# Gated linear attention into a squared-ReLU MLP on one core: the first two pairs of chunks handled differently, and the order of work planned anew

## The chip, the core and the metric

The kernel runs on one core of one Trainium2 chip. A core has five engines that run their own instruction streams and meet at semaphores: TensorE (PE; its weight loads are listed apart as PEld), VectorE (DVE), ScalarE (ACT), GpSimd (POOL) and SyncE (SP), which here only issues transfers. The metric is the device time of one launch in microseconds (us). Before the change three runs took 174.03, 174.82 and 174.83 us, so the median is 174.82.

## The reference

Four batches of eight heads go through a recurrence over 768 steps with 48 channels a head. The result, 3072 rows of 384, goes through an MLP with a squared ReLU.

```python
def _attn_ref(q, k, v, alpha) -> np.ndarray:
    for t in range(S):
        state = alpha[:, :, t, :, None] * state + np.einsum('bhd,bhe->bhde', k[:, :, t], v[:, :, t])
        y[:, :, t] = np.einsum('bhd,bhde->bhe', q[:, :, t], state)

def _moe_ref(x, w_in, w_out) -> np.ndarray:
    h = x @ w_in                      # 384 -> 2048
    r = np.maximum(h, 0.0)
    return ((r * r) @ w_out).astype(np.float32)   # 2048 -> 384
```

All inputs and the output are float32; the kernel multiplies in bf16 and accumulates in float32.

## The kernel before, in words

**Tiling.** The 3072 steps are cut into chunks of 128, and two chunks make a *pair* (`g`, 0 to 11; three pairs to a batch). Instead of stepping through time the kernel works on a whole chunk: decays become running sums of logarithms, the part inside a chunk is a masked product of q and k, and the part from earlier chunks comes from a state of 48 by 48 a head that is carried on.

**Stages of a pair.**
- *loads*: alpha, k, q and v into `RAW` (line 596).
- *decay*: logarithm on ACT, running sums by matmuls with triangles of ones on PE, exponentials on ACT into `ASB`, scaling of k and q on DVE into `QKS`, and the cast of v into `VBF` (`values`, line 617). Pairs 0 and 1 do this by halves of the heads (`decay_half`, line 669).
- *turned*: the scaled q and k are transposed into `QKT`. Pairs 0 to 3 do it on PE, with an eviction from PSUM by ACT or DVE (`turned_half`, line 732, for pairs 0 and 1), the later ones by a transposing DMA.
- *scores*: products of q and k, masked into `PMB`. A mask is applied by DVE directly from PSUM (L797), or ACT first copies the bank to SBUF and DVE multiplies from there (L790 and L792). Which of a pair's four masks go the second way is in `COPIED`.
- *carry*: end products, k times v over each of the two chunks (L816, line 805), from which DVE or POOL makes the next states (L831, L834, L837).
- *mixed*: masked scores times v, plus q times the states (L856), evicted into `XT`. In the later pairs the result is turned back by a DMA.
- *up*: eight units a pair, of six matmuls each (L985), with a ReLU on ACT (L995) and the square on DVE (L997).
- *down*: two groups of 16 matmuls a pair, one for each chunk (`tt`, L1018), evicted by ACT (L1025) and stored.

**Transfers.** SP issues most loads. POOL's queue has the weights in nine pieces: first six (five of `WIN`, in cuts 2, 2, 4, 4 and 4 of 16 columns blocks, then one of `WOUT`), gated on the landing of pair 1's alpha (`PARTS`), then the loads of pair 2 (`QUEUED`), then the last three pieces of `WOUT`.

**The order.** Every operation has a priority: `TABLE` gives an offset for each stage of each pair, `2 * g` is added, and lower comes first. PSUM banks and dependencies are drawn in the order of the stages' priorities, from the pools that `POOLS` names: 0 is four banks, 1 adds `psO0`, 2 adds three more. Then `Program.order` runs the engines through a model in which an engine that is free takes the lowest priority among what is ready, and writes the order down; on the chip it is fixed. The model holds durations, and also the arrival of PE's instructions: they come in blocks of `BLOCK` = 254, the first boundary 56 earlier, and a block is there `FETCH` after the one before was begun, less `CALM` outside a busy period. Where PE would idle before the first down, `fill` puts matmuls on a constant tile (L1004), and 28 of them open the program.

**Banks of the MLP.** The ups alternate between two banks, `psH0` and `psH1`; the first `WIDE` of them may also use `psO0`, which is the accumulator of each pair's first down group.

Of the kernel before, what the change touches and what calls it, by code (L numbers as in the profile page):

```python
# [16 lines left out]
    dict(decay0=-97.00571, decay1=-78.81219, turned0=-80.03886, turned1=-50.01967, scores0=-30.48193, scores1=-47.68772, carry=-27.42287, mixed=-10.34508, up=13.54943, down=5.38323, scale00=46.21211, scale01=15.6952, scale10=-43.7223, scale11=24.38742, ends=-0.19963, values=-0.27295, loads=-207.65325, pair=-201.56601, last=-192.65267),  # L17
    dict(decay0=-75.64812, decay1=-42.50964, turned0=-47.6396, turned1=-36.35059, scores0=-27.54796, scores1=-14.27818, carry=-27.02336, mixed=-9.92749, up=13.91788, down=5.77749, scale00=24.25062, scale01=-73.05864, scale10=28.44156, scale11=53.47468, ends=69.1898, values=-2.51561, loads=-194.30495, pair=-191.20832, last=-172.89529),
    dict(decay=-7.48475, turned=3.12884, scores0=9.47855, scores1=6.55405, carry=1.85699, mixed=10.59462, up=17.47201, down=3.43096, loads=-74.75818),
    dict(decay=9.05655, turned=9.43988, scores0=10.08163, scores1=11.32914, carry=10.39665, mixed=11.89133, up=17.92099, down=4.23853, loads=-73.80479),  # L20
    dict(decay=9.3345, turned=9.43988, scores0=11.74226, scores1=10.89073, carry=10.54465, mixed=12.03376, up=21.0863, down=1.87816, loads=-73.8231),
    dict(decay=8.7564, turned=9.67304, scores0=11.70712, scores1=12.0564, carry=10.89438, mixed=12.21007, up=21.29448, down=1.43236, loads=6.43356),
    dict(decay=8.69387, turned=9.58387, scores0=11.86871, scores1=11.0227, carry=10.77621, mixed=11.96308, up=21.05913, down=2.40841, loads=7.7569),
    dict(decay=9.23435, turned=10.31244, scores0=11.36545, scores1=11.31146, carry=10.85231, mixed=12.13782, up=22.61627, down=2.40841, loads=8.07049),
    dict(decay=9.1013, turned=10.6921, scores0=11.60211, scores1=13.72977, carry=10.17742, mixed=18.09191, up=22.49685, down=2.4227, loads=7.9898),
    dict(decay=9.1013, turned=10.66148, scores0=19.46122, scores1=19.67082, carry=16.52927, mixed=20.05528, up=26.04938, down=2.38036, loads=7.9898),
    dict(decay=17.68176, turned=18.97432, scores0=20.03114, scores1=21.47118, carry=18.7218, mixed=19.83455, up=26.32882, down=2.72559, loads=13.16964, masks=-27.17958),
    dict(decay=17.68176, turned=18.97432, scores0=20.03114, scores1=21.47118, carry=18.7218, mixed=19.83455, up=26.32882, down=2.72559, loads=13.16964),
]
POOLS = [dict(decay=1, turned=2, scores=2, carry=1, mixed=2), dict(decay=0, turned=1, scores=1, carry=1, mixed=0)]  # L30
WEIGHTS = (-75.27555, -73.28278)
TURNED = (0, 1, 2, 3)
BACK = (4, 5, 6, 7, 8, 9, 10, 11)
BEHIND = {6: 4, 7: 6, 8: 6, 9: 7, 10: 7, 11: 9}
RUNS = {10: 16}
WARMUP = (28, 1)
WIDE = 10
# [27 lines left out]
class Program:  # L65
# [1146 lines left out]
```

## Time and profile before

| what | value |
|---|---|
| median of three runs | 174.82 us (174.03 to 174.83) |
| the profiled execution | 174.21 us |
| its span, from first to last instruction | 172.5 us |
| PE busy | 167.6 us, 97% |
| DVE busy | 119.4 us, 69% |
| ACT busy | 116.9 us, 68% |
| POOL busy | 36.4 us, 21% |
| matmuls | 2611 |
| granted TensorE clock | full speed in all slices |

Rows of a profile have the engine, a line of the kernel (L985 is line 985), what is written and read, how many instructions, and times. In the table by stretches a row has the stretch, its length, then busy time and number of instructions of PE, PEld, DVE, ACT and POOL, then granted clock, the share of the DMA engines and GB/s. In the chain of waits and the timeline a row begins with its start and its length in us. A bracket names the idle time ahead of an instruction and what ended it; "issue" means that the profile shows nothing that the engine waited for. In a row for one line, three numbers with slashes are minimum, median and maximum in ns.

### The profile page before, as it was taken

The page shows a single profiled execution, that of the slowest core. Times are in us where ns is not written, and L with a number is a line of the kernel's source. Part 1 is how long each engine was busy: PE and PEld are TensorE (multiplying, and loading weights), DVE is VectorE, ACT ScalarE, POOL GpSimd, SP SyncE. Part 2 cuts the span into 40 slices and gives each one's busy share as a digit, 9 for nine tenths or more (in the row PEclk, how much of TensorE's full clock was granted, in tenths as well). Part 3 has the DMA queues.
Part 4 walks back from the last instruction along what each step waited for, and adds up shares of the span by engine and source line. Part 5 has one row for each costly group of instructions (what it writes and reads, how often), then busy time and mean ns, then how long its engine had stood idle before and what let it go on. Part 6 is the DMA issues. An engine that isn't in the chain of part 4 may idle for free.

```text
span 172.5 us, 6016 instructions
## 1 busy us (share of the span) xinstructions
PE 167.6 (97%) x2611; PEld 123.9 (72%) x2611; DVE 119.4 (69%) x257; ACT 116.9 (68%) x236; POOL 36.4 (21%) x63
## 2 busy tenths in 40 slices
PE   7889999999999999999999999999999999999994
PEld 7457687757777786777777777777776867877763
DVE  7887958964999999578897698289784804423300
ACT  2887679546989685568993794669973556657621
POOL 4079600100012001010142122320512310202220
PEclk9999999999999999999999999999999999999999
DMA  5999999999994999999999999999929343112122
GB/s 138 323 304 171 206 324 238 157 270 287 308 327 113 230 217 261 144 305 196 323 203 234 218 207 252 236 231 332 186 50 160 72 62 62 22 25 49 40 51 91
DMA packets 76314, 32.89 MB, mean 191 GB/s; under 512 B 69632, under 2 KB 75456, under 8 KB 76288
## 3 DMA queue, kind: packets, MB, share of 16 engines
q1 hardware_dynamic: 70384, 25.04, 65.0%
q0 software_dynamic: 5904, 7.47, 21.8%
q8 instruction: 20, 0.33, 0.8%
q14 instruction: 6, 0.05, 0.1%
HBM read 25.17 MB, written 4.72 MB: 173 GB/s over the span
## 4 chain that ended last, share of the span: by engine, by line
PE 95%; DVE 2%; issue 1%; ACT 0%
PE psH L985 36%; PE psO L1018 36%; PE psG L777 4%; PE psO L1004 3%; PE psG L856 2%; PE psG L942 2%; PE psG L816 2%; PE psO L1037 2%; PE psG L932 2%; PE psO L985 2%; DVE qks L696 2%; PE psG L642 1%; PE psG L715 1%; PE psG L681 1%; PE psH L856 1%
## 5 line engine op out<-in xcount | busy, mean ns | idle before, releaser
L995 ACT ACTIVATE rr<-psH 128x512 bf16<-128x512 f32 x92 | 55.3, 612 | 22.6 <-PE psH L985 20.6
L985 PE MATMUL psH<-xt,win 128*128 128x256 bf16 x552 | 70.5, 273 | 0.0
L1018 PE MATMUL psO<-wout,gt 128*128 128x384 bf16 x368 | 70.0, 326 | 0.0
L985 PEld LDWEIGHTS psH<-xt,win 128*128 128x128 bf16 x552 | 52.7, 98 | 11.6 <-DVE xt L900 0.2
L997 DVE TENSOR_TENSOR gt<-rr 128x512 bf16<-128x512 bf16 x96 | 40.3, 434 | 29.6 <-ACT rr L995 29.3
L1018 PEld LDWEIGHTS psO<-wout,gt 128*128 128x128 bf16 x368 | 34.3, 98 | 17.8 <-ACT osb L1025 0.3
L797 DVE TENSOR_TENSOR pm<-psG,mask 128x512 bf16<-128x512 f32 x44 | 27.9, 682 | 3.7 <-PE psG L777 2.9
L971 POOL DMA_DIRECT2D out_dram<-osb x28 | 15.0, 541 | 47.4 <-ACT osb L1025 47.4
L837 POOL TENSOR_TENSOR sbf<-ust,acp 128x192 bf16<-128x192 f32 x13 | 9.0, 689 | 75.3 <-DVE ust L834 75.2
L1025 ACT ACTIVATE osb<-psO 128x384 f32<-128x384 f32 x23 | 11.3, 492 | 14.6 <-PE psO L1018 14.3
L663 DVE TENSOR_TENSOR qks<-raw,asb 128x768 bf16<-128x768 f32 x20 | 18.7, 966 | 2.0 <-ACT asb L652 2.0
L632 DVE TENSOR_TENSOR raw<-raw 128x384 f32<-128x384 f32 x20 | 11.0, 564 | 0.0
L624 ACT ACTIVATE vbf<-raw 128x768 bf16<-128x768 f32 x12 | 10.1, 842 | 0.0
L652 ACT ACTIVATE asb<-psG 128x384 bf16<-128x384 f32 x20 | 9.9, 497 | 0.2
L958 ACT ACTIVATE yb<-psG 128x384 bf16<-128x384 f32 x14 | 6.2, 489 | 4.4 <-PE psG L932 4.4
L777 PEld LDWEIGHTS psG<-qkt 64*64 64x64 bf16 x360 | 5.7, 106 | 4.0 <-issue 2.8
L1004 PE MATMUL psO<-warm 128*128 128x128 bf16 (+1 forms) x41 | 7.4, 347 | 1.1 <-DVE warm L523 1.1
L777 PE MATMUL psG<-qkt 64*64 64x128 bf16 x360 | 8.3, 220 | 0.1
L632 DVE TENSOR_TENSOR raw<-raw,ro 128x384 f32<-128x384 f32 x10 | 5.5, 551 | 0.8 <-DMA raw<-in_q_dram 0.5
L648 ACT ACTIVATE ro<-raw 128x384 f32<-128x384 f32 x10 | 5.2, 524 | 0.6 <-DMA raw<-in_alpha_dram 0.6
L834 DVE TENSOR_TENSOR ust<-psG,sbf 128x192 f32<-128x192 f32 x14 | 4.9, 353 | 0.7 <-POOL sbf L837 0.4
L654 ACT ACTIVATE ro<-ro 128x384 f32<-128x384 f32 x10 | 5.2, 524 | 0.1
(104 smaller groups left out, 137.2 us busy)
## 6 DMA issues: line engine op xcount, KB each, us to landing
raw<-in_alpha_dram SPq DMA_DIRECT2D x11, 384.0 KB, 4.8
raw<-in_k_dram SPq DMA_DIRECT2D x11, 384.0 KB, 5.0
raw<-in_q_dram SPq DMA_DIRECT2D x11, 384.0 KB, 5.6
raw<-in_v_dram SPq DMA_DIRECT2D x11, 384.0 KB, 5.9
out_dram<-osb POOLq DMA_DIRECT2D x28, 96.0 KB, 2.6
out_dram<-osb SPq DMA_DIRECT2D x9, 192.0 KB, 3.9
wout<-in_moe_w_out_dram POOLq DMA_DIRECT2D x4, 384.0 KB, 13.6
win<-in_moe_w_in_dram POOLq DMA_DIRECT2D x3, 384.0 KB, 8.8
```

Of the source, the lines that this page charges most:

```text
L624: add("ACT", lambda act: act.activation(dst, src, AF.Copy), 740, at, reads=raw(r, 2), writes=[("vbf", vb)])
L632: add("DVE", lambda e: e.tensor_tensor(dst, a0, a1, ALU.mult), 470, at_, reads=reads, writes=writes, port=True)
L663: add("DVE", lambda dve, z=z, decays=decays: dve.tensor_tensor(QKS[x][:, z, :, :, 0:D], both(r, z), decays, ALU.mult), 870, at + 0.05 + 0. ...
L777: last = pe.matmul(banks[i, j // 2][0][64 * c:64 * c + 64, col:col + 128].rearrange("p (a b) -> p a b", a=2), QKT[t][64 * i:64 * i + 64, 0 ...
L797: add("DVE", lambda dve, i=i, X=X, ps=ps: dve.tensor_tensor(PMB[m][:, i, 2 * X:2 * X + 2].rearrange("p j n s -> p j (n s)"), ps[:].rearran ...
L971: add(by, lambda e, dst=dst, ps=ps: e.dma_start(dst, OSB[o][ps, :]), 600, at + 0.01 * i, reads=[("osb", o)], dma=("own" if by == "POOL" el ...
L985: last = pe.matmul(ps[:, f * TW:(f + 1) * TW].rearrange("p (c t) -> p c t", c=2), WIN[:, kt, fj * 128:(fj + 1) * 128], XT[:, 2 * (g % NX): ...
L995: add("ACT", lambda act: act.activation(ro, ri, AF.Relu), 480, at, reads=[key], writes=[key, ("rr", r)])
L997: add("DVE", lambda dve: dve.tensor_tensor(gt[:, 2 * u:2 * u + 2, :], rr, rr, ALU.mult), 340, at, reads=[("rr", r)], writes=[("gt", g % NG ...
L1004: last = pe.matmul(psO[1][:, 0:128 * wide].rearrange("p (a b) -> p a b", a=wide), WARM[:], bass.AP(tensor=WARM, offset=0, ap=[[128, 128], ...
L1018: last = pe.matmul(ps[:, 0:DM], GT[g % NGT][:, fj, tt * 128:(tt + 1) * 128], WOUT[:, fj, :], start=(fj == 0), stop=(fj == FT - 1))
L1025: add("ACT", lambda act: act.activation(OSB[o][:], ps[:, 0:DM], AF.Copy), 372, at, reads=[key], writes=[key, ("osb", o)])
```

## The change

What it does:
- `COPIED`: two masks of each of the first two pairs go through an ACT eviction, where it was one.
- `CASTS`: pair 0's cast of v goes from ACT to POOL. `TURNS`: the second half of pair 1's transposes is evicted by DVE, where it was ACT.
- `PARTED`: pair 1's carry is issued as two operations, one for each chunk, each with a priority and a pool of its own. `HALVED` could split the masked product of mixed in the same way, but is off for both pairs.
- `POOLS` has an entry for each half.
- `WIDE` is 16, so all ups of pairs 0 and 1 may use `psO0`.
- `BEHIND`: the loads of pairs 9 and 11 are no longer held behind a transpose, those of 10 are. `OWN`: q of pair 10 is loaded through POOL's queue.
- The model's blocks come later: `FETCH` 5900 for 5200, `CALM` 2200 for 1500. All priorities are new, and so is the order in the whole program.

```diff
-    dict(decay0=-97.00571, ... scores0=-30.48193, scores1=-47.68772, carry=-27.42287, mixed=-10.34508, up=13.54943, ...),
-    dict(decay0=-75.64812, ... scores0=-27.54796, scores1=-14.27818, carry=-27.02336, mixed=-9.92749, up=13.91788, ...),
+    dict(decay0=-146.86488, ... scores0=-97.39775, scores1=-60.74046, carry=-78.79402, mixed=-43.93218, up=-29.78865, ..., carry1=-9.28472),
+    dict(decay0=-76.01398, ... scores0=-34.45505, scores1=-34.33621, carry=-68.21069, mixed=-30.58997, up=-27.20524, ..., carry1=-32.02976),
...
-POOLS = [dict(decay=1, turned=2, scores=2, carry=1, mixed=2), dict(decay=0, turned=1, scores=1, carry=1, mixed=0)]
-WEIGHTS = (-75.27555, -73.28278)
+POOLS = [dict(decay0=1, decay1=2, turned0=1, turned1=1, scores0=0, scores1=0, carry=1, carry1=0, mixed=2), dict(decay0=2, decay1=2, turned0=2, turned1=1, scores0=0, scores1=0, carry=2, carry1=0, mixed=2)]
+WEIGHTS = (-161.5303, -133.27356)
-BEHIND = {6: 4, 7: 6, 8: 6, 9: 7, 10: 7, 11: 9}
+BEHIND = {6: 4, 7: 6, 8: 6, 10: 8}
-WIDE = 10
+WIDE = 16
-CASTS = ('ACT', 'ACT')
+CASTS = ('POOL', 'ACT')
-COPIED = ((1,), (2,))
-TURNS = ('DVE', 'ACT')
+COPIED = ((0, 2), (0, 1))
+TURNS = ('DVE', 'DVE')
+PARTED = (0, 1)
+HALVED = (0, 0)
+OWN = ((10, 1),)
...
-    BLOCK, AHEAD_OF_ALL, FETCH, CALM, BUSY_FROM, BUSY_UNTIL = 254, 56.0, 5200.0, 1500.0, 11200.0, 31000.0
+    BLOCK, AHEAD_OF_ALL, FETCH, CALM, BUSY_FROM, BUSY_UNTIL = 254, 56.0, 5900.0, 2200.0, 11200.0, 31000.0
...
+            if (g, j) in OWN:
+                add("POOL", lambda e, s=s, dst=dst: e.dma_start(dst, s), 950, at + 0.1 * (j != 3),
+                    writes=raw(r, j), dma=f"rawq{r}_{j}", nbytes=TW * HD * 4, rate=pr.LATER, tardy=g >= FIRST)
+                continue
...
-    def carry(g, at, spots=None):
+    def carry(g, at, spots=None, part=None):
         first, final = g % NW == 0, g % NW == NW - 1
-        chunks = [0] if final else [0, 1]
+        chunks = [0] if final else [0, 1] if part is None else [part]
+        name = "carry1" if part else "carry"
...
+            if g < FIRST and PARTED[g]:
+                for c in range(2):
+                    stage(2 * g + o["carry1" if c else "carry"], lambda at, g=g, c=c: carry(g, at, None, c), "carry", g, c)
+            else:
+                stage(2 * g + o["carry"], lambda at, g=g: carry(g, at), "carry", g)
```

More of the change, by code (lines that the diff above doesn't have):

```diff
@@ L19 @@
[L19 to L26, printed above, removed]
@@ new lines @@
+    dict(decay0=-76.01398, decay1=-71.34874, turned0=-46.31235, turned1=-38.30092, scores0=-34.45505, scores1=-34.33621, carry=-68.21069, mixed=-30.58997, up=-27.20524, down=10.34217, scale00=-28.77031, scale01=9.28326, scale10=52.36844, scale11=42.61829, ends=-1.25386, values=-13.06113, loads=-168.76464, pair=-167.45514, last=-149.62032, carry1=-32.02976),
+    dict(decay=-33.84237, turned=-32.51282, scores0=-20.86174, scores1=-31.33323, carry=-19.71539, mixed=-19.02679, up=11.43945, down=16.45818, loads=-136.74137),
@@ L768, in scores @@
         halves = sorted({j // 2 for j in js})
-        banks = {(i, X): bank(POOLS[g]["scores"] if g < FIRST else 0) for X in halves for i in range(2)}
+        banks = {(i, X): bank(POOLS[g]["scores%d" % X] if g < FIRST else 0) for X in halves for i in range(2)}
         def mm(pe):
@@ L820, in mm @@
             return last
-        add("PE", mm, 250, at, reads=[("qks", x, 0, X) for X in range(2)] + [("vbf", vb)],
-            writes=[b[1] for b in banks], form=64, size=32 * len(chunks))
+        add("PE", mm, 250 if part is None else 260, at, reads=[("qks", x, 0, X) for X in range(2)] + [("vbf", vb)],
+            writes=[b[1] for b in banks.values()], form=64, size=32 * len(chunks))
         for c in chunks:
@@ L1116, in bass_gla_recurrent__then__act_relu_squared_kernel @@
             ahead(("decay", g, 0), [("decay", g, 1)])
+            if PARTED[g]:
+                ahead(("carry", g, 0), [("carry", g, 1)])
         ahead(("turned", g), [("decay", g + NQK)])
```

41 lines of the change are left out of this document (27 added, 14 removed).

## The prediction

> **What bounds the kernel now.** I read the page first (busy shares, slices), then the table by stretches, the chain of waits over the first 35 us, and then the rows of single lines. The page:
>
> ```profile
> PE 167.6 (97%) x2611; PEld 123.9 (72%) x2611; DVE 119.4 (69%) x257; ACT 116.9 (68%) x236; POOL 36.4 (21%) x63
> PE   7889999999999999999999999999999999999994
> win<-in_moe_w_in_dram POOLq DMA_DIRECT2D x3, 384.0 KB, 8.8
> ```
>
> PE is the bound. The slices show it below nine tenths only in the first three and in the last, so nothing that speeds another engine up in the middle shortens the run: the change can win only PE time that is idle or spent on filler early, or lose what it adds to PE. The stretches say where that is (us; busy and number of instructions by engine):
>
> ```profile
> 5.08:12.20 7.12, 6.18 (x88) 3.75 (x88) 5.94 (x14) 6.69 (x16) 2.70 (x4) 1.00 1.17 323
> 12.20:16.74 4.54, 4.44 (x159) 3.02 (x160) 3.41 (x9) 3.39 (x6) 4.54 (x6) 1.00 1.24 176
> 16.74:22.30 5.56, 5.21 (x110) 3.89 (x114) 4.70 (x12) 2.77 (x5) 3.33 (x5) 1.00 1.26 206
> 22.30:32.60 10.30, 10.30 (x115) 8.39 (x115) 8.11 (x18) 9.91 (x20) 0.00 (x0) 1.00 1.19 268
> ```
>
> From 22.30 PE is busy 10.30 of 10.30. Ahead of that, part of "busy" is filler (line 1004). The chain of waits (start, length):
>
> ```profile
> 14.43 0.37 PE psG L816 x32
> 14.80 0.54 PE psO L1004 x2
> 16.06 0.32 PE psO L1004
> 16.74 0.83 PE psH L985 x6
> 20.66 0.32 issue
> 20.98 0.59 PE psG L856 x28
> 21.57 0.76 PE psH L985 x6
> 22.33 0.29 PE psG L856 x12
> ```
>
> The first up (line 985) begins at 16.74. Two fillers, 0.54 and 0.32 us, stand where PE waits for the first pair's end products: carry (L816) runs at 14.43 although its inputs are old, then DVE makes the state. At 20.66 PE stops for 0.32 with no releaser. The counts of instructions explain that stop:
>
> ```profile
> 0.00:9.75 9.75, 8.05 (x94) 5.73 (x98) 7.45 (x30) 6.15 (x13) 2.15 (x10) 1.00 0.88 241
> 0.00:15.40 15.40, 13.31 (x222) 9.10 (x225) 12.04 (x40) 11.16 (x23) 7.80 (x17) 1.00 1.01 240
> 0.00:20.40 20.40, 18.27 (x345) 12.77 (x349) 16.88 (x52) 14.08 (x27) 12.47 (x22) 1.00 1.06 230
> 20.98 0.42 PE L856 MATMUL psG<-pm,vbf 64*64 64x128 bf16 x16 [0.32 <-issue]
> ```
>
> Matmuls and weight loads together are 192, 447 and 694 at 9.75, 15.40 and 20.40: steps of 255 and 247, which with a few waits is the 254 of the planner's BLOCK. So PE stood at the end of a block of instructions, and the next came at 20.98, 20.98 - 15.40 = 5.58 us after the one before was begun. The old planner reckoned with 5.2 (FETCH), the new one with 5.9. Blocks are thus a second limit on this stretch. The third is the weights:
>
> ```profile
> L579 POOL DMA_DIRECT2D win<-in_moe_w_in_dram x5: 772/772/909, 9.5 to 12.7; - x5
> DMA to landing us min/median/max: 5.3/6.5/9.6
> ```
>
> First piece: 9.5 + 5.3 = 14.8. The third large one is issued at 12.7 and lands 9.6 later, 22.3; the middle one about 12.0 + 8.8 = 20.8. Pieces one to three feed four ups, and the fifth (21.57) cannot start before 20.8, however early everything else is. If PE had all other work of the two pairs behind it by then, it would win 21.57 + 0.29 - 20.8 = 1.06 us (0.29 is what the chain still runs at 22.33). That is the ceiling, unless the weights come sooner, and their place in POOL's queue and their gate (alpha of pair 1) stay.
>
> **The change, part by part.**
>
> ```profile
> 8.52 0.85 ACT L624 ACTIVATE vbf<-raw 128x768 bf16<-128x768 f32 x1
> 15.20 1.03 ACT L758 ACTIVATE qkt<-psG 128x1024 bf16<-128x1024 bf16 x1
> 10.14 0.61 ACT L790 ACTIVATE rr<-psH 128x512 bf16<-128x512 f32 x1
> 11.01 0.68 DVE L797 TENSOR_TENSOR pm<-psO,mask 128x512 bf16<-128x512 f32 x1
> 12.54 0.42 DVE L792 TENSOR_TENSOR pm<-rr,mask 128x512 bf16<-128x512 bf16 x1
> 14.87 0.36 DVE L831 TENSOR_TENSOR sbf<-psG,acp 128x192 bf16<-128x192 f32 x1 [0.97 <-PE psG L816]
> L720 DVE COPY qkt<-psG x4: 680/683/692, 33.2 to 45.7; 128x1024 bf16<-128x1024 bf16 x4
> ```
>
> *ACT and DVE of the first pairs* (COPIED, TURNS, CASTS). Each pair has a second mask by eviction: ACT +0.61 each, DVE 0.68 becomes 0.42. The second half of pair 1's transposes goes from ACT (1.03) to DVE (0.68 by the same shape on L720). Pair 0's cast of v leaves ACT (0.85). ACT: 2 x 0.61 - 1.03 - 0.85 = -0.66; DVE: 0.68 - 2 x 0.26 = +0.16. On the path this is taken at 0: DVE's +0.16 has the 0.97 of idle ahead of L831 as its cover (without it, 0.16 is lost), and ACT, which idles after 16.23 until the first relu, is not what PE waits for.
>
> *The cast on POOL.* No row shows it. Nearest rows:
>
> ```profile
> L542 POOL TENSOR_SCALAR_AFFINE_SELECT mask<-mask x2: 411/413/415, 2.7 to 3.1; 64x256 bf16<-64x256 bf16 x2
> L530 POOL TENSOR_SCALAR_AFFINE_SELECT hexc<-hexc x1: 286/286/286, 1.9 to 1.9; 128x128 bf16<-128x128 bf16 x1
> L837 POOL TENSOR_TENSOR sbf<-ust,acp x13: 504/642/1218, 33.0 to 134.9; 128x192 bf16<-128x192 f32 x13
> L696 DVE TENSOR_TENSOR qks<-raw,asb x4: 550/554/558, 6.3 to 7.8; 128x384 bf16<-128x384 f32 x4
> 9.50 4.00 POOL L579 DMA_DIRECT2D win<-in_moe_w_in_dram  x5 [5.95 <-DMA raw<-in_alpha_dram]
> ```
>
> One-input instructions cost 286 ns for 128 elements and 413 for 256, 127 ns per 128 more: 768 elements come to 0.29 + 5 x 0.127 = 0.92 us. By the two-input L837, 768/192 x 0.642 = 2.57. I take 0.92 as one input is nearer, and keep 0.92 to 2.57. The cast waits for the four scalings on DVE (the last starts at 7.8 and takes 0.55: 8.4), so it ends at 9.3, just inside POOL's idle time before 9.50. Cost 0; carry then has its v at 9.3, as now (8.52 + 0.85). Behind it in POOL's queue stand all weights and the loads of pair 2; past 9.50 each microsecond delays them.
> The Trainium skill, page "GPSIMD Engine Reference", section "Engine selection", holds one-input work on that engine to be roughly at line rate and two-input work about twice as slow as on VectorE. The sum by it is the one with 0.92; no run here shows this cast.
>
> *Carry and mixed of pair 0 earlier.* In the table carry of pair 0 now stands right behind the first half of its scores and ahead of pair 1's transposes; its banks are drawn before theirs. Then the state is there when the masks are, the end products follow the masked product without the fillers, and the first ups go up to where weights allow: -0.54 - 0.32 = -0.86. Ends: 0 (DVE gives the state no sooner) and -1.06 (the ceiling).
>
> *Blocks.* The order made for 5.9 should not run into the 0.32 stop. But 64 carry instructions moved forward also bring PE to the next boundary sooner, and the two intervals here, 5.65 and 5.58, are both near a block's time. Between -0.32 and +0.3 I take 0.
>
> *Pair 1's carry by chunk* (PARTED). One carry of 32 matmuls becomes two of 16. Pair 2's carry already has one chunk:
>
> ```profile
> 32.15 0.36 PE psG L816 x16
> 32.52 1.00 PE psG L715 x16
> ```
>
> Sixteen cost 0.36, the 32 above 0.37: the split buys no PE time and adds 0.36. It gives the state that mixed of pair 1 needs earlier. Taken in full, since its priority puts it ahead of most ups and nearly all of PE is taken up there: +0.36; ends 0 (in filler time) and 0.56 (with two changes of form at about 0.1: 16 transposes from 32.52 take 1.00).
>
> *Third bank for 16 ups* (WIDE). All of pairs 0 and 1's ups may use psO0, so pair 0's first down stands behind the last of them; ACT evicts for them:
>
> ```profile
> sum 8.00, ACT 7.68; mean ACT 1.92
> ```
>
> That is 24 to 32 us: ACT is at 96% there with the same 12 relus and pair 2's decay. Taken at 0, as wout's later pieces are not yet there either; if the cover of two downs goes, 2 x 0.65 of PE work is missing for a while.
>
> *Later table, BEHIND, OWN.* Loads of 9 and 11 no longer wait in SP's queue behind a transpose, 10 does; q of pair 10 is issued by POOL (0.9 us there by its loads of pair 2, 1.15 saved on SP). POOL is 21% busy; cover is the ups of earlier pairs. 0. The order of the dense part changes only how often PE changes between small and full matmuls, at 0.1 a change: three visits more or fewer are 0.6 either way.
>
> **Sum.** The profiled execution took 174.21 us, span 172.5 and 1.71 around it; it is near the lowest of the runs (median 174.82, 174.03 to 174.83). 174.21 - 0.86 + 0.36 = 173.7.
>
> **Rivals.**
> *A, forecast*: 173.7, own range 172.8 (ceiling 1.06 with the split free, and 0.4 of changes saved) to 174.3.
> *B, hidden*: pair 1's mixed still ends at about 22 because the blocks come every 5.6 us from 9.75 on and its masks wait on DVE. Then the gained 0.86 is waited out at 20.8: 174.2. For it: steps of 255 and 247. Against: the end of one block is reached earlier when the waits shrink.
> *C, slower*: the cast takes POOL 2.57. It ends at 8.4 + 2.57 = 10.97, and weights move by 1.47; u4 has 0.77 of slack (21.57 - 20.8), so PE loses 0.7, the split's 0.36 stays: 174.21 + 1.06 = 175.3, and up to 176.5 if the carry waits too. It decides once the cast is over 1.1 + 0.8 = 1.9 us. For it: L837's 1218 ns at most. Against: its one input.
> By the Trainium skill, page "SBUF — State Buffer", section "SBUF: two separate sides", a GpSimd instruction and a VectorE one with two SBUF inputs lock each other out for the whole instruction. By that rule the cast would also hold up the scalings of pair 0 or the products from evicted masks, at most its own length; the spread of L837, 504 to 1218, agrees with such a lock and does not prove it.
> *D, ACT bound*: 16 ups ahead of the first down, ACT at 96%, one down of 0.65 without cover: 174.3.
> *The change not doing what it says*: HALVED is (0, 0), so the split of mixed is dead code.
>
> **How the numbers follow.** 0.5% is about what a measurement can tell from no change: 0.87 us, taken around 174.5, between the profiled time and the median. A 0.43 (faster 0.26, same 0.17), B 0.20 (0.04, 0.14, slower 0.02), C 0.23 (same 0.04, slower 0.19), D 0.14 (0.01, 0.08, 0.05). Faster 0.31, same 0.43, slower 0.26. The range reaches from A's low end to C's price with what the changes of form can add: 172.8 to 175.6.
>
> **What would show it.** Right: L624 of pair 0 on POOL at about 0.9 us from 8.4, line 579 still at 9.5; L816 of pair 0 before 11; first L985 before 16; no filler between 14.5 and 20; fifth up at 20.8 to 21.2; two L816 of 16 in pair 1. Wrong: line 579 after 10; PE "issue" of over 0.3 before 21; idle PE between 22 and 35; or fewer or more changes of form later, with the total PE time off by over 0.6.

## The result, and the profile after

The changed kernel took 176.28 us (median of 22 runs, 175.23 to 181.53) against 174.82 (22 runs, 173.91 to 176.33) in the same sitting: the ratio is 1.0078, 95% interval [1.0053, 1.0103]. It is slower, by about 0.8%. The forecast was 173.7, in a range of 172.8 to 175.6. Medians and ranges here and below are over all executions, while the ratios leave out a slower state that some executions fall into, so a ratio is not always the quotient of the two medians.

The profiled execution took 176.06 us with a span of 174.3, against 174.21 and 172.5. The page of the changed kernel, busy shares and PE's slices:

```profile
PE 167.5 (96%) x2609; PEld 124.1 (71%) x2609; DVE 119.7 (69%) x258; ACT 115.9 (67%) x236; POOL 39.1 (22%) x65
PE   7888999999999999799999999999999999999994
```

PE's busy time is that of before (167.5 against 167.6), and the span grew by 1.8 us in which PE is idle. The busy time hides two things: the real matmuls are the same in number and form, but there are 11 long fillers where there were 13. New low slices are the fourth, from 13 to 17 us, and the seventeenth, from 70 to 74 us. PE's waits in the changed kernel (releaser, sum in us, times, longest):

```profile
PE psO L754 <- DVE qks L703: 1.1, 1, 1.1
...
PE psG L784 <- DMA qkt<-qks: 1.0, 1, 1.0
...
PE psO L1034 <- DMA wout<-in_moe_w_out_dram: 0.4, 1, 0.4
```

The first is in the stage that the change is about, the last behind it, and the second (L784, scores) is far from both. A second look at the same kernel on another chip, the first experiment, tells which of them belong to the kernel. Its list has the second alone, at 69.90; what else it lists is 0.2 or the warm-up at the start:

```profile
PE psO L1020 <- DVE warm L526: 1.1, 1, 1.1
PE psG L784 <- DMA qkt<-qks: 0.7, 1, 0.7
...
```

That execution took 174.94 us. In the first the idle 1.09 came from q of pair 1, which was late for DVE; the timeline shows it one step earlier:

```profile
12.90 0.56 DVE L703 TENSOR_TENSOR qks<-raw,asb 128x384 bf16<-128x384 f32 x1 [0.88 <-DMA raw<-in_q_dram]
```

No other profile with this order of the first pairs has a wait of that size there: the longest single one is 0.4, in eight further kernels below and in the second execution. So I take the second execution for the kernel's own course, and 1.09 and 0.4 for an accident of the first. It was one of the shorter executions, though (median 175.31 in its sitting), so an ordinary one loses some tenths more than it shows. The stretch from 60 to 80 us, in the changed kernel, in its second execution, and in the kernel before:

```profile
60.00:80.00 20.00, 19.02 (x374) 14.04 (x363) 16.07 (x31) 13.07 (x29) 3.69 (x3) 1.00 0.91 188
```

```profile
60.00:80.00 20.00, 19.25 (x364) 14.03 (x362) 16.30 (x32) 13.99 (x30) 3.69 (x3) 1.00 0.95 190
```

```profile
60.00:80.00 20.00, 20.00 (x381) 14.40 (x371) 16.60 (x33) 13.04 (x28) 1.13 (x2) 1.00 1.11 223
```

Before, PE had no gap there; after, 0.98 and 0.75 us. How the distance to the kernel before builds up is seen when both traces are compared at the same amount of matmul work. Each matmul counts with a fixed length for its form (109 ns an up, 162 a down of 384 columns, 56 a transpose, 15 the small ones), warm-up and filler are left out, and the rows give how many us later than in the profile of before the same sum is reached:

```
work (us)            12     26     45     55     65     100    155
time before          23.7   38.0   57.4   67.4   78.0   112.8  168.6
changed, first      +0.19  +0.62  +0.91  +1.05  +1.76  +1.97  +1.85
changed, second     -0.19  -0.30  -0.01  +0.14  +0.62  +0.84  +0.72
```

The second row is the finding: the first pairs win 0.2 to 0.3 us, and at the end the kernel is 0.72 behind, so the dense part loses 1.0. Of this 0.75 is the gap at 70. The other 0.27 has no gap: PE is busy that much longer with the same matmuls. The columns from 45 to 100 hang on the lengths assumed and move by some tenths with others, as the two orders do different work first; the first two columns and the last do not.

**The first pairs.** The chain of waits of the second execution:

```profile
15.09 0.35 PE psG L824 x16
15.44 0.32 PE psO L1020
15.77 0.83 PE psH L1001 x6
16.60 0.45 PE psG L754 x8
17.05 0.36 PE psG L824 x16
17.41 0.76 PE psO L1001 x6
...
20.61 0.20 issue
...
21.38 0.76 PE psO L1001 x6
```

and rows of the chain before:

```profile
13.88 0.55 PE psG L747 x8
...
17.57 0.66 PE psO L985 x6
18.23 0.35 PE psG L777 x16
18.57 0.76 PE psH L985 x6
```

The first up starts at 15.77 (before 16.74), 0.97 earlier, but this is mostly a change of places. Eight transposes of pair 1 and its second group of sixteen end products stood ahead of the first up; now they stand behind it (16.60 and 17.05, together 0.81). The second up starts at 17.41 (17.57), 0.16 earlier, and PE comes to the end of its block of instructions at 20.61 (20.66), 0.05 earlier, with four ups done in both kernels. There it stops with no releaser, as before, and the next block comes at 20.80 (20.98). The fifth up starts at 21.38 (21.57): 0.19 earlier, most of it because the stop is shorter. A filler still stands at 15.44, right ahead of the first up.

The cast on POOL, in the changed kernel:

```profile
8.48 0.82 POOL L628 CAST vbf<-raw 128x768 bf16<-128x768 f32 x1 [4.92 <-DVE qks L703]
9.82 4.01 POOL L582 DMA_DIRECT2D win<-in_moe_w_in_dram  x5 [0.52 <-DMA raw<-in_alpha_dram]
```

It takes 0.82 us, and the weights behind it wait for pair 1's alpha, not for the cast.

**The gap at 70 us.** Rows of the changed kernel's timeline that lead to pair 5's scores:

```profile
56.07 0.52 ACT L645 ACTIVATE lab<-raw 128x384 bf16<-128x384 f32 x1
59.52 0.64 PE L784 MATMUL psG<-qkt 64*64 64x128 bf16 x32
61.41 0.33 PE L649 MATMUL psG<-lab,hinc 128*128 128x384 bf16 x1
64.91 1.71 SPq L734 DMA_TRANSPOSE qkt<-qks  x1
71.05 0.64 PE L784 MATMUL psG<-qkt 64*64 64x128 bf16 x32 [0.97 <-DMA qkt<-qks]
```

and the same steps before:

```profile
54.66 0.33 PE L642 MATMUL psG<-lab,hinc 128*128 128x384 bf16 x1
59.21 4.44 SPq L727 DMA_TRANSPOSE qkt<-qks  x1
59.59 0.64 PE L777 MATMUL psG<-qkt 64*64 64x128 bf16 x32
67.64 0.64 PE L777 MATMUL psG<-qkt 64*64 64x128 bf16 x32
```

Pair 5's logarithm is there at 56.6, but its running sums stand behind pair 4's scores in the new order (61.41 behind 59.52), where they stood ahead of them (54.66 ahead of 59.59). So the transposing DMA is issued at 64.91 instead of 59.21, and lands when PE has already come for it.

### The profile page after: what moved, and what is told of

Read it like the earlier page. It is cut to its first block, busy times and chain, and to the rows that moved or that the text cites. A ratio compares the mean times of both kernels' runs of the same rounds, so it can differ in the third digit from the quotient of the medians.

```text
span 174.3 us, 6001 instructions
## 1 busy us (share of the span) xinstructions
PE 167.5 (96%) x2609; PEld 124.1 (71%) x2609; DVE 119.7 (69%) x258; ACT 115.9 (67%) x236; POOL 39.1 (22%) x65
## 4 chain that ended last, share of the span: by engine, by line
PE 74%; DMA 14%; POOL 5%; DVE 3%; SPq 2%; issue 0%; ACT 0%
PE psO L1034 32%; PE psH L1001 29%; DMA wout<-in_moe_w_out_dram 8%; DMA qkt<-qks 3%; PE psG L784 3%; DMA raw<-in_alpha_dram 3%; POOL win L582 2%; POOL raw L608 2%; SPq L616 2%; PE psG L958 2%; PE psO L1053 2%; DVE pm L804 1%; PE psG L824 1%; PE psG L864 1%; PE psG L948 1%; PE psG L722 1%
## 5 line engine op out<-in xcount | busy, mean ns | idle before, releaser
L1001 PE MATMUL psH<-xt,win 128*128 128x256 bf16 x546 | 69.1, 273 | 0.1
L1034 PE MATMUL psO<-wout,gt 128*128 128x384 bf16 x368 | 68.6, 326 | 0.4 <-DMA wout<-in_moe_w_out_dram 0.4
L1001 PEld LDWEIGHTS psH<-xt,win 128*128 128x128 bf16 x546 | 51.9, 98 | 10.6 <-DVE xt L916 0.4
L845 POOL TENSOR_TENSOR sbf<-ust,acp 128x192 bf16<-128x192 f32 x13 | 9.8, 757 | 71.0 <-DVE ust L842 71.0
L639 DVE TENSOR_TENSOR raw<-raw 128x384 f32<-128x384 f32 x20 | 11.7, 600 | 0.1
L784 PE MATMUL psG<-qkt 64*64 64x128 bf16 x384 | 8.7, 219 | 1.2 <-DMA qkt<-qks 1.0
L784 PEld LDWEIGHTS psG<-qkt 64*64 64x64 bf16 x384 | 6.1, 106 | 4.8 <-issue 1.9
L631 ACT ACTIVATE vbf<-raw 128x768 bf16<-128x768 f32 x11 | 9.4, 851 | 0.0
L1020 PE MATMUL psO<-warm 128*128 128x128 bf16 (+1 forms) x39 | 6.9, 345 | 1.1 <-DVE warm L526 1.1
L824 PE MATMUL psG<-vbf,qks 64*64 64x48 bf16 x288 | 5.5, 188 | 0.0
L645 ACT ACTIVATE lab<-raw 128x384 bf16<-128x384 f32 x10 | 5.3, 526 | 0.2 <-DVE raw L639 0.2
```

What stands on the lines that cost most here:

```text
L639: add("DVE", lambda e: e.tensor_tensor(dst, a0, a1, ALU.mult), 470, at_, reads=reads, writes=writes, port=True)
L784: last = pe.matmul(banks[i, j // 2][0][64 * c:64 * c + 64, col:col + 128].rearrange("p (a b) -> p a b", a=2), QKT[t][64 * i:64 * i + 64, 0 ...
L845: add(by, lambda e, u=u, to=to, ac=ac: e.tensor_tensor(to, UST[u][:], ac, ALU.mult), 600 if by == "POOL" else 270, at + 0.05 * c, reads=[( ...
L1001: last = pe.matmul(ps[:, f * TW:(f + 1) * TW].rearrange("p (c t) -> p c t", c=2), WIN[:, kt, fj * 128:(fj + 1) * 128], XT[:, 2 * (g % NX): ...
L1034: last = pe.matmul(ps[:, 0:DM], GT[g % NGT][:, fj, tt * 128:(tt + 1) * 128], WOUT[:, fj, :], start=(fj == 0), stop=(fj == FT - 1))
```

## Experiments

All ratios are to the kernel before, run on the same chip in the same call. A fence with rows is of the experiment's own profile.

**The changed kernel again.** No edit.

> The changed kernel once more, to see which of its waits come back. In its first profile PE stood 1.09 us at 13.5 (for the scaling of pair 1, whose q landed at 12.81 where it was 11.62), 0.36 at 32.05 (for wout), 0.97 at 71.05 (for the transposing DMA of pair 5). Theory 'dense order' (the new order of the later pairs leaves less room between the transposing DMAs and the scores that need them): the wait at 71 comes back, of 0.5 to 1.5 us, in the same place. Rival 'accident' (one late transfer in one execution): it is gone or elsewhere, and the span is 173 or less. Ratio to the kernel before 1.005 to 1.010 either way.

175.31 us (174.57 to 181.38), ratio 1.0061 [1.0034, 1.0087]; read above. The loss stands without the disturbance of the first pairs, and the table has it in the dense part.

**New pairs, old rest.** The later rows of the table, `WIDE`, `BEHIND`, `WEIGHTS` and `OWN` as before, and the ups and downs of the first two pairs as well.

```diff
-WIDE = 16
+WIDE = 10
-OWN = ((10, 1),)
+OWN = ()
...
-    dict(decay=-33.84237, turned=-32.51282, ...
+    dict(decay=-7.48475, turned=3.12884, ...
```

> The stages of pairs 0 and 1 as changed (two masks by eviction, cast on POOL, split carry, their priorities and pools), all later priorities, the ups and downs, WIDE, BEHIND and OWN as before; planned with the later blocks. 'Dense order': the loss goes with the rest, so this stands at the old time plus what the first 30 us cost, 0.2: ratio 0.998 to 1.003, no wait for a transposing DMA over 0.3. Rival 'first pairs' (the new pairs make transfers late by 1 us, and that goes on to the end): ratio 1.004 to 1.008, and wout's second piece lands at 32 again, not at 30.8.

176.67 us, 1.0149 [1.0121, 1.0178]: slower than the whole change, which neither theory expected.

```profile
22.69 0.83 PE L1001 MATMUL psH<-xt,win 128*128 128x256 bf16 x6 [0.17 <-ACT xt L919]
...
90.53 0.64 PE L784 MATMUL psG<-qkt 64*64 64x128 bf16 x32 [1.22 <-DMA qkt<-qks]
```

The third up starts at 22.69, and at equal work the kernel is about 2 us behind at 38 us: the old priorities of the ups do not place them among the new stages, so the mixture is bad in its own way. A wait of 1.22 for the transposing DMA of pair 7 comes on top. Here the later table is the old one, so such waits are not peculiar to the new one; 'dense order' had expected none over 0.3.

**Old pairs, new rest.** The opposite: stages, pools and engines of the first two pairs as before (priorities shifted by 100 so that they still come first), all else new.

```diff
-COPIED = ((0, 2), (0, 1))
-TURNS = ('DVE', 'DVE')
-PARTED = (0, 1)
+COPIED = ((1,), (2,))
+TURNS = ('DVE', 'ACT')
+PARTED = (0, 0)
```

> The other way round: the stages of pairs 0 and 1 with the old priorities (all shifted by the same amount), one mask by eviction, cast on ACT, one carry; everything later as changed. 'Dense order': ratio 1.006 to 1.010, with a wait of PE for a transposing DMA of 0.5 or more. 'First pairs': ratio 0.998 to 1.003.

177.61 us, 1.0187 [1.0151, 1.0222]. Its profile is of the longest of its runs (180.67), so I read only its time. It agrees in sign with a loss in the new rest, but the size shows that the halves of a plan made as a whole do not add up. Later experiments therefore change single places.

**The cast back on ACT.** PE's order stays.

```diff
-CASTS = ('POOL', 'ACT')
+CASTS = ('ACT', 'ACT')
```

> The changed kernel with pair 0's cast of v back on ACT; PE's order comes out the same, only the cast's place on ACT and POOL differs. In the changed kernel the cast took 0.82 us on POOL from 8.48 and was over before alpha of pair 1 landed (9.53), so theory 'cast is free': same time as the changed kernel (ratio of the two 0.997 to 1.003), line 579/582 still issued 0.3 after alpha's landing. Rival C of the prediction (the cast delays the weights): faster than the changed kernel by 0.5 us or more.

176.99 us (173.89 to 182.93, 12 runs), 1.0033 [0.9992, 1.0074]. The runs scatter too far to tell it from the change; the cast's engine is not shown to matter in either direction. In its profile (177.44 us), with the order of the change on PE, PE waits 0.52 for the transposing DMA of pair 5 and 1.79 for that of pair 6, which lands 8.9 us after its issue.

**Fewer instructions ahead of everything.** In the changed kernel the warm-up is 14 matmuls of 256 columns instead of 28 of 128: 28 PE instructions fewer (a matmul and its load count as two), same length, same order. Every boundary between blocks of instructions comes 28 instructions later in the order.

```diff
-    add("PE", lambda pe: busy(pe, WARMUP[0], WARMUP[1]), 2950, -6, ...
+    add("PE", lambda pe: busy(pe, WARMUP[0] // 2, 2), 2950, -6, ...
```

> The changed kernel, the same order on every engine, but the warm-up is 14 matmuls of 256 columns where it was 28 of 128: the same PE time, 28 PE instructions fewer, so every boundary between blocks of 254 instructions comes 28 instructions later. In both looks at the changed kernel PE crosses a boundary (instruction 2230) six instructions ahead of pair 5's scores (2236), the fetch of a block starts at 69.15 and 68.00, and the transposing DMA of pair 5 ends 1.85 us after that, its 16 shares 1.8 and 1.25 apart instead of 0.1. Theory 'block collides': with the boundary behind the scores the shares end within 0.3 of each other, PE's wait for pair 5 (0.97 and 0.75) falls under 0.2, and the kernel gets 0.5 to 0.9 us faster: 1.000 to 1.003 of the kernel before. Rival 'late issue' (the transpose is issued at 64 to 65 and needs 6 us anyhow): wait and time stay, 1.005 to 1.008.

175.54 us, 1.0067 [1.0042, 1.0091].

```profile
21.36 0.36 PE L864 MATMUL psG<-qkt,sbf 64*64 64x128 bf16 x12 [0.88 <-issue]
77.38 0.64 PE L784 MATMUL psG<-qkt 64*64 64x128 bf16 x32 [0.72 <-DMA qkt<-qks]
```

The wait at pair 5 is gone and one at pair 6 has come, and the stop at the block is longer, as PE is there earlier and the block is not. Nothing is won.

**Twelve fewer.** The same with 16 matmuls of 128 and 6 of 256.

```diff
+    add("PE", lambda pe: (busy(pe, 16, 1), busy(pe, 6, 2))[1], 2950, -6, ...
```

> The changed kernel, order unchanged, with 12 PE instructions fewer in the warm-up (16 matmuls of 128 columns and 6 of 256). With 28 fewer the transpose of pair 5 landed undisturbed, but the next boundary came to lie 36 instructions ahead of pair 6's scores and that transpose landed 1.4 us apart, with a wait of 0.71. With 12 fewer the boundaries lie 6 instructions behind pair 5's scores and 80 and more ahead of pair 6's. 'Block collides': shares of both transposes within 0.4, PE's waits for the two together under 0.3, time 0.3 to 0.6 us under the changed kernel: 1.002 to 1.004 of the kernel before. Rival 'late issue': a wait of 0.5 or more for pair 5 or 6 as in all looks so far, 1.005 to 1.008.

175.09 us, 1.0032 [1.0007, 1.0056]. This pair of profiles shows most directly what delays pair 5. Pair 5's transposing DMA in the second execution of the changed kernel, with the row of the instruction queue between 64 and 68.2 us (packets, MB, share of 16 engines):

```profile
L734 SPq DMA_TRANSPOSE qkt<-qks x1: 1711/1711/1711, 64.0 to 64.0; - x1
DMA to landing us min/median/max: 5.9/5.9/5.9
q8 instruction: 1, 0.02, 1.4%
```

and with twelve instructions fewer, where the same stretch has no row of that queue:

```profile
L734 SPq DMA_TRANSPOSE qkt<-qks x1: 1710/1710/1710, 63.9 to 63.9; - x1
DMA to landing us min/median/max: 4.3/4.3/4.3
20.78 0.31 PE L864 MATMUL psG<-pm,vbf 64*64 64x128 bf16 x8 [0.42 <-issue]
77.24 0.64 PE L784 MATMUL psG<-qkt 64*64 64x128 bf16 x32 [1.05 <-DMA qkt<-qks]
```

Same issue, same time of issue. With a fetch of instructions in its way (one packet of 0.02 MB, 1.4% of 16 engines over 4.2 us, so 0.94 us of one of them) the DMA lands 5.9 us after its issue, without it 4.3. The wait of pair 5 is gone, and pair 6 waits 1.05, where the two together were expected under 0.3. At the third block PE stops 0.42, 0.22 more than with the twelve instructions, and goes on at the same time (20.78 and 20.80).

**And pair 6's scores one group of ups later.** The kernel of the twelve fewer, with one swap in PE's order: six ups stand ahead of pair 6's scores that stood behind them.

```diff
-    dict(decay=18.64729, turned=19.18678, scores0=21.16774, scores1=21.15596, ...
+    dict(decay=18.64729, turned=19.18678, scores0=21.96774, scores1=21.95596, ...
```

> The kernel of the twelve fewer instructions (changed kernel, six of the warm-up matmuls twice as wide), with the scores of pair 6 put one group of six ups (0.8 us) later in PE's order by 0.8 in their priority; nothing else on PE, ACT, POOL and SP changes place. If the waits for the transposing DMAs are what is lost in the dense part, the wait of 1.05 at pair 6 falls to 0.3 or less, the end of the profile comes 0.6 to 0.9 us earlier, and the ratio goes from 1.003 to 0.997 to 1.000. If the time is lost anyway (the landing moves with the scores, or the next pair waits in its place), the ratio stays at 1.002 to 1.006 and a wait of 0.5 or more stands at L784 or L864 behind 76 us.

174.66 us (174.25 to 175.32, 12 runs), 1.0017 [0.9992, 1.0042]. PE waits for no transposing DMA any more:

```profile
18.85 1.48 PE L1001 MATMUL psH<-xt,win 128*128 128x256 bf16 x12 [0.39 <-DMA win<-in_moe_w_in_dram]
21.29 0.31 PE L864 MATMUL psG<-pm,vbf 64*64 64x128 bf16 x8 [0.28 <-issue]
...
77.45 0.64 PE L784 MATMUL psG<-qkt 64*64 64x128 bf16 x32
```

Pair 6's DMA still lands 7.6 us after its issue at 69.82, so PE comes for it with nothing to spare. From 1.0061 to 1.0032 to 1.0017 the ratio falls by 0.0044, 0.77 us, with two edits that change no work. All three intervals overlap, so the steps rest on the traces more than on the times. The ratio is not within the expected 0.997 to 1.000, and the profile ends 0.4 us earlier than that of the twelve fewer, not 0.6 to 0.9. At equal work it is 0.1 behind the kernel before at 38 us, as the weights (0.39) and the block (0.28) take what the first pairs won, and 0.5 at the end; in between PE is busy 0.29 longer.

**Pair 5's decay earlier.** In the changed kernel its priority goes from 28.98 to 27.0, ahead of pair 4's scores.

```diff
-    dict(decay=18.97711, turned=20.91717, ...
+    dict(decay=17.0, turned=20.91717, ...
```

> The changed kernel with one number of the table another: the decay of pair 5 has priority 27.0 where it was 28.98, so it draws its PSUM bank ahead of pair 4's scores, as it did before the change, and not from them. In the changed kernel its sums run at 61.4 although their logarithm is there at 56.6, for the bank that pair 4's last mask frees. Theory 'late issue': sums at 57 to 59, the transposing DMA issued by 62 (64.9 and 64.0 now, 59.2 before), no wait of PE for pair 5 and 0.5 to 0.9 us less: 1.000 to 1.003 of the kernel before. Rival 'block collides' alone: the wait goes only if the boundary's place goes too, which it does here as the order shifts, so this run cannot speak against it, but the shares' spread can be read. Rival 'the order as a whole': another wait of 0.5 or more turns up elsewhere and the ratio stays at 1.005 or above.

176.98 us, 1.0153 [1.0129, 1.0177]. Pair 5's transposing DMA goes out at 59.2 and PE does not wait for it.

```profile
76.90 0.64 PE L784 MATMUL psG<-qkt 64*64 64x128 bf16 x32 [0.89 <-DMA qkt<-qks]
```

Pair 6 waits instead, and the order around it changed too: at equal work it is 0.3 us ahead of the kernel before at 38 us and 2.5 behind at the end, and only 0.89 of that is a wait. The rest is PE busy 2.0 longer; from 38 us on it goes 60 times between matmuls on 128 rows and on 64, where it went 44 times in the kernel before. One priority in a dense plan moves much else.

**Both.** That priority and the 14 wider warm-up matmuls.

```diff
-    dict(decay=18.97711, turned=20.91717, ...
+    dict(decay=17.0, turned=20.91717, ...
...
+    add("PE", lambda pe: busy(pe, WARMUP[0] // 2, 2), 2950, -6, ...
```

> The changed kernel with both: pair 5's decay at 27.0 and the wide warm-up. If the two theories name two costs that can each be taken away, this is the fastest of the four; with the 0.2 to 0.3 us that the first 38 us win in an undisturbed execution it would come to 0.997 to 1.001 of the kernel before. If it is no faster than either alone, they were one cost.

176.89 us, 1.0134 [1.0107, 1.0162]; pair 6 still waits 0.88, at 77.08.

**The old kernel with a late pair 5.** In the kernel before, the decay of pair 5 goes behind pair 4's scores.

```diff
-    dict(decay=8.7564, turned=9.67304, ...
+    dict(decay=9.9, turned=10.2, ...
```

> The kernel before with two numbers of the table another: decay of pair 5 at 19.9 (18.76) and its transpose at 20.2 (19.67), behind pair 4's scores, as in the changed kernel. 'Late issue': the transposing DMA of pair 5 goes out 2 us or more later than at 59.2, PE waits for it or has nothing to spare, and the time rises by 0.3 to 1.0 us: 1.002 to 1.006. 'Block collides' and 'the order as a whole': within 0.2% of the kernel before, unless a boundary falls on it.

176.35 us, 1.0106 [1.0084, 1.0128]. The gap appears in the old kernel, at the same pair and of the same size, and a second one at pair 7:

```profile
70.37 0.64 PE L777 MATMUL psG<-qkt 64*64 64x128 bf16 x32 [0.75 <-DMA qkt<-qks]
92.99 0.64 PE L777 MATMUL psG<-qkt 64*64 64x128 bf16 x32 [0.76 <-DMA qkt<-qks]
```

None of the new first pairs is in this kernel. The late place of one decay is enough for a loss as large as the change's. It is more than the expected 1.002 to 1.006: besides the two waits PE is busy 1.0 us longer from 38 us on, with 52 such changes instead of 44.

**The loads back.** The changed kernel with `BEHIND` and `OWN` of before.

```diff
-BEHIND = {6: 4, 7: 6, 8: 6, 10: 8}
+BEHIND = {6: 4, 7: 6, 8: 6, 9: 7, 10: 7, 11: 9}
-OWN = ((10, 1),)
+OWN = ()
```

> The changed kernel with BEHIND and OWN as before (loads of 9 and 11 held behind a transpose again, q of pair 10 through SP), planned anew; PE's order is the same for the first 198 groups of matmuls, and differs in 145 lines behind them. If the places of the loads make the transposing DMAs of pairs 5 and 6 late, they land at least 0.7 us ahead of their scores (L784 without a wait over 0.3 between 60 and 80 us), and the ratio to the kernel before falls to 1.000 or below. If the table's order does it, the loads make no difference: a wait of 0.5 to 1.0 us at L784 between 65 and 80 stays, or the time is lost at another pair, and the ratio is 1.004 to 1.010.

176.02 us, 1.0105 [1.0077, 1.0133], and the wait is where it was:

```profile
69.78 0.64 PE L784 MATMUL psG<-qkt 64*64 64x128 bf16 x32 [0.69 <-DMA qkt<-qks]
```

So the places of the loads do not make it.

**The third bank back.** `WIDE` 10 in the changed kernel.

```diff
-WIDE = 16
+WIDE = 10
```

> The changed kernel with WIDE 10 for 16 (the first ten ups alone may use the third bank), planned anew: downs of pair 0 come among the ups of pair 1. Theory: the third bank costs nothing by itself, and the loss sits at the transposing DMAs, so the ratio stays at 1.004 to 1.010 with a wait of 0.5 to 1.0 at L784 between 65 and 80 us. Rival (the bank): with 16 ups ahead of the first down, ACT's relus and the squares set the pace between 24 and 36 us, the lag at 38 us falls by 0.3 or more and the ratio falls to 1.003 or below.

178.73 us, 1.0237 [1.0202, 1.0272]: both sides missed.

```profile
31.45 0.83 PE L1001 MATMUL psH<-xt,win 128*128 128x256 bf16 x6 [0.50 <-ACT rr L1011]
52.78 0.86 PE L864 MATMUL psG<-pm,vbf 64*64 64x128 bf16 x48 [1.16 <-DVE pm L804]
```

In this order the ups need the third bank: with ten of them on it PE waits for ACT's ReLU at 31, and with the downs then in other places for a mask at 52.8. Pairs 5 and 6 do not wait here, so their gap is one of several that an order can have.

**The old kernel with wider warm-up**, 14 of 256 and then 7 of 512 (28 and 42 instructions fewer), so that PE has more work to do ahead of the boundary, to see whether the block then comes without a stop.

```diff
+    add("PE", lambda pe: busy(pe, WARMUP[0] // 2, 2), 2950, -6, ...
```

> The kernel before, order unchanged, with the same 28 PE instructions fewer (14 warm-up matmuls of 256). The third boundary, at which PE stood from 20.44 to 20.99, comes 28 instructions later. Theory 'a block has its own time' (the third arrives at 20.7 to 21.7 whenever PE reaches the boundary ahead of it: so in all ten profiles): PE does 14 matmuls more ahead of the stop, the stop shrinks by about 0.2, and with no new collision the kernel is 0.1 to 0.3 us faster: 0.998 to 1.000. Rival 'the block comes a fixed time after the last boundary': the stop stays at 0.5, ratio 1.000. A transposing DMA with shares over 1 us apart and a wait at its scores would add 0.5 to 1.

174.60 us, 1.0015 [0.9994, 1.0035]. Its profile is of its longest run (175.89): PE waits 0.41 for weights at the third up, stops 0.74 at the block and goes on at 22.57.

```diff
+    add("PE", lambda pe: busy(pe, WARMUP[0] // 4, 4), 2950, -6, ...
```

> The kernel before with 42 PE instructions fewer (7 warm-up matmuls of 512 columns). 'A block has its own time': the stop at the third boundary shrinks by 0.3 or goes, 0.997 to 0.999 if no transposing DMA is hit, and this would be a version that beats both kernels. If one is hit, 1.002 to 1.005, and the trace shows at which pair.

174.57 us, 1.003 [1.0006, 1.0055]. The stop at the third block is not shorter, it is longer:

```profile
21.31 0.30 PE L856 MATMUL psG<-qkt,sbf 64*64 64x128 bf16 x7 [0.53 <-issue]
```

From there to the end PE runs 0.04 us behind the kernel before. In this kernel, work that is brought ahead of the boundary is waited out at it.

**The old kernel planned with later blocks.** Only `FETCH` and `CALM` of the change.

```diff
-    BLOCK, AHEAD_OF_ALL, FETCH, CALM, BUSY_FROM, BUSY_UNTIL = 254, 56.0, 5200.0, 1500.0, 11200.0, 31000.0
+    BLOCK, AHEAD_OF_ALL, FETCH, CALM, BUSY_FROM, BUSY_UNTIL = 254, 56.0, 5900.0, 2200.0, 11200.0, 31000.0
```

> The kernel before with the planner's FETCH and CALM of the change (5900 and 2200) and nothing else; the order comes out different in some 170 lines on PE. Theory 'the order as a whole' (small shifts of the order cost waits for transposing DMAs): 1.002 to 1.008, with at least one wait of 0.5 for a transpose. Rival 'better model, better order': no stop at the third boundary and 0.996 to 0.999.

175.14 us, 1.0052 [1.0034, 1.0069].

```profile
30.93 0.82 PE L1018 MATMUL psO<-wout,gt 128*128 128x384 bf16 x4 [0.31 <-DMA wout<-in_moe_w_out_dram]
```

The stop at the block is not among its waits. But the first down now comes to `WOUT` before it has landed, and at the end the kernel is 1.0 behind without a further gap: PE is busy 0.7 longer from 38 us on, with 51 such changes instead of 44. Later blocks in the model alone do not make a better order.

## Why the prediction was wrong

Two steps failed. *Carry and mixed of pair 0 earlier* was put at -0.86, while all the first pairs together brought 0.2 to 0.3 us, and *Later table* was put at 0 and cost 1.0.

**What bounds the kernel** was read rightly: PE, and ahead of 22 us blocks and weights too. What was not read was how near other limits lay in the stretches where PE is busy 10.30 of 10.30.

**Cast on POOL**: right. 0.82 us against the estimate of 0.92, weights not held by it; rival C is refuted. The Trainium skill, page "GPSIMD Engine Reference", section "Engine selection", has one-input work there roughly at line rate; the 0.82 agrees with that.

**ACT and DVE of the first pairs**, at 0: no wait for them above 0.2 us in the undisturbed execution, so nothing speaks against it; fillers may cover shorter ones.

**Carry and mixed of pair 0 earlier**, -0.86: this step failed. Pair 0's carry is done before 10, and in the second execution the first up starts before 16, as the prediction's marks had it. But two other marks failed: a filler still stands at 15.44, and the fifth up comes at 21.38, not at 20.8 to 21.2. The step took the three fillers between 12 and 16.7 for time that would be saved up to the block. At the block PE was 0.05 us earlier than before, as shown above: what stood ahead of the first up moved behind it, and PE is still without work at other places. Rival B, with a chance of 0.20, had the gain made and then waited out at the block; the block can have taken no more than its stop, 0.20, in this execution. It takes more in profiles where PE comes to it earlier (0.42 and 0.88 above). The weights show in two profiles (0.39 and 0.41).

**Blocks**, taken at 0 between -0.32 and +0.3: in the second execution the stop is 0.20 instead of 0.32, within these bounds. In the variants of the new order it reaches 0.88, outside them.

**Pair 1's carry by chunk**, +0.36: the size is right (0.35 and 0.36 for sixteen each, 0.37 for 32 before), and the second sixteen stand between the first two ups, where PE is busy. Whether PE would gain it without the split, or wait longer at the block, no run tells.

**Third bank for 16 ups**, at 0: not shown to cost anything; without it this order loses more.

**Later table, BEHIND, OWN**, at 0 with 0.6 either way by changes of form: this is the step that decided the sign. It measured about +1.0: from -0.30 at 38 us to +0.72 at the end. Of this 0.75 is the wait for pair 5's transposing DMA. The step left out that an order also sets how far ahead of their use transfers are issued. Nothing in the text looked at the distance from a transposing DMA to its scores, although its row in the profile of before has landings from 4.4 to 8.5 us after the issue:

```profile
L727 SPq DMA_TRANSPOSE qkt<-qks x8: 1762/3566/5103, 54.0 to 128.1; - x8
...
DMA to landing us min/median/max: 4.4/5.7/8.5
```

An order that issues at 64.9 what is wanted at 70.1 (71.05 less 0.97) leaves 5.2 us, inside that scatter. The list of what would show the prediction wrong had idle PE between 22 and 35, and so looked in the wrong place. No rival had this mechanism; D and C put their losses elsewhere.

The other 0.27 is what the step did name, changes of form, within its 0.6 either way. From the point at which 26 us of work are done, this is how often PE goes from matmuls on 128 rows to such on 64 or back, and how long it is busy without its gaps:

```
                                     changes   PE busy (us)
new pairs, old rest                    43        131.42
kernel before                          44        131.54
changed, first and second              46        131.79, 131.81
loads back                             48        132.29
third bank back                        49        132.35
old, later blocks                      51        132.24
old, late pair 5                       52        132.55
pair 5 earlier                         60        133.52
```

Each change more goes with 0.10 to 0.19 us. The rows of the chain before show one side of it: six ups take 0.66 right behind other ups (17.57) and 0.76 behind scores (18.57). No run changes this number alone, so the cause is read from these rows and not tested.

The sum thus comes out as -0.30 in the first pairs, +0.75 for the wait and +0.27 in busier PE, +0.72 in all, where -0.50 was forecast. (Rival D's own sum comes to 174.4, not 174.3; nothing hangs on it.)

**Open.** The two edits that take the waits away lower the ratio by some 0.77 us, with overlapping intervals. What an ordinary execution of the changed kernel loses beyond the second profile was not traced. Why pair 6's DMA takes 7.6 to 7.9 us in several of these runs was not settled. Neither was why the new order scatters more (to 181.5 us).

## What to carry to other kernels

When an order is planned anew, read for every transfer of the dense part how long before its use it lands, and how much its landing scatters from one to the next; a plan that is as dense but spends that distance loses at the first collision. Count also how often PE changes between forms of matmuls, as this is lost without any gap. Before crediting work that is brought forward, compare both orders where the same work is done: an operation that starts earlier may only have changed places with another. Then look for the next thing that comes at its own time (a block of instructions, a weight), where a gain can be waited out. The worth of a part of such a plan can't be measured by mixing it with the other plan; small edits that keep PE's order can be read, and swaps of single groups.

## What the runs showed of the hardware that was not expected

**PE stops at a fixed count of instructions, and more work ahead of the stop does not take the stop away.** In all thirteen profiles that show the third stop it stands after 698 or 699 matmuls and weight loads, also with 12, 28 or 42 instructions fewer in the warm-up. PE's restart behind it: 20.80 in the changed kernel, 20.78 with twelve instructions fewer, 21.36 with 28 fewer, 21.29 with twelve fewer and the swap; 20.98 in the kernel before, 21.31 with 42 fewer, 22.57 with 28 fewer. PE stopped for 0.20, 0.42, 0.88, 0.28, 0.32, 0.53 and 0.74 us. In none of the five with fewer instructions did the block come more than 0.02 us earlier, and in four of them it came 0.33 to 1.59 us later. What sets its arrival is open; the DMA engines are loaded then, but no run changed their load.

**A fetch of instructions delays a transposing DMA by 1.1 to 1.8 us.** In eight profiles pair 5's goes out between 63.9 and 65.3. In four of them (the changed kernel twice, the loads back, the old kernel with a late pair 5) a packet of the instruction queue starts 2.0 to 4.2 us after the issue, and the DMA lands 6.1, 5.9, 5.8 and 5.4 us after it. In the other four (28 fewer, twelve fewer, the swap, the third bank back) none starts between issue and landing but one just at the issue, and it lands after 4.3 in each. The packet has 0.02 MB and holds one DMA engine for about 1 us. Twelve instructions at the start of the program, some 60 us earlier, decided whether the two met. It is not the only cause of a late landing: pair 6's took 6.9 us in the second execution with no such packet between.
